# Turns of gathered rows bound behind a low part, a step sooner, and two more units by quarter rows: linear attention with a mixture of experts

## The chip, the cores and the metric

The kernel runs on one core of a Trainium2 chip. The metric is the device time of one execution in microseconds. Before the change it is 872.87 us, the median of three runs (872.1 to 873.55).

## The reference

```python
def phi(x):                                  # attention features, per head
    proj = x @ w_phi                         # 64 -> 128
    proj = proj - max(abs(proj), axis=-1)
    return concat([exp(proj), exp(-proj)])   # 256 features
q_p, k_p = phi(q), phi(k)                    # 8 x 8 heads, 576 tokens, head 64
x = (q_p @ (k_p.T @ v)) / (q_p @ sum(k_p) + 1e-6)      # -> [4608 tokens, 512]
logits = x @ w_gate                          # 8 experts
e = argmax(logits); gate = softmax(logits)[e]
out = gate * (relu(x @ w1[e]) @ w2[e])       # 512 -> 1024 -> 512, one expert per token
```

Everything is float32, with inputs and result of that type.

## The kernel before

The first part (up to about 400 us) computes the attention and writes its rows to `x_dram` in HBM, with the gate weights in `g_dram`. It also sorts the tokens by expert into blocks of 128, of which 41 are always computed. The second part runs the expert over these blocks. Blocks 0 to 37 go in pairs of one expert: pair unit `u` (0 to 18) holds blocks `2u` and `2u+1`. Blocks 38, 39 and 40 are the single units 19, 20 and 21.

Products keep float32 precision by splitting each operand into a high part (`wh`, `xh`, `hh`: a cast on ScalarE, ACT) and a low part (`wl`, `xl`, `hl`: a subtraction on VectorE, DVE), and by three matmuls on TensorE (PE): high by high, high by low, low by high. A pair unit has four steps `j` = 0 to 3. In each, `pair_first(u, j)` is 24 matmuls into the PSUM tile `pm` (two in flight), then `hh` on ScalarE and `hl` on VectorE; `pair_second` of the step before is 12 matmuls into `po`. A `po` matmul with `hl` (L1198) follows two that need `hh` alone. After the last step ScalarE scales both `po` by the gate into `ob`, and GpSimd (POOL) scatters them to `out`.

Rows of a block come to the tile `xg` (four of them) by indirect DMAs from POOL's queue. Early units take whole rows of 512 elements with one DMA per block (index `gidx`), later ones take a row in four quarters (index `qidx`), with four DMAs per block. `by_quarters(u)` says which. `x_parts(u, i)` then turns the block: without quarters by four PE transposes into the PSUM tile `px` (L1157), with quarters by one 32x32 block transpose on VectorE (L1152). From `px` come `xh` and `xl`.

In the loop over `u` the fetches for unit `u+2` are issued in unit `u`, divided over the steps by `cuts`; each waits for that step's `hh` (`paced`). `lined` keeps the order of row fetches and scatters in the pair loop as written. `behind(m, other)` only fixes that `m` stands after `other` on its engine. The rest of each engine's order is set by the scheduler that builds the program, by what is ready in its own model of time. So a turn of unit `u+2`, written in unit `u+1`, can stand one unit earlier than it is written, right behind its own fetches. Every engine runs its queue in order.

Of the kernel before, what the change touches and what calls it, by code (L numbers as in the profile page):

```python
# [14 lines left out]
ALU = mybir.AluOpType  # L15
# [30 lines left out]
KD = DM // P  # L46
# [10 lines left out]
def tile_linear_attention_moe(  # L57
# [12 lines left out]
    V, A, G, T = nc.vector, nc.scalar, nc.gpsimd, nc.tensor  # L70
# [189 lines left out]
    def behind(m, other):  # L260

        tc.add_manual_dep(
            m.ins,
            other.ins.name,
            mybir.DependencyInfo(mybir.DependencyClass.NoSync, mybir.DependencyReason.DATA),
            reason="order of the engine",
        )
# [796 lines left out]
    st = {}  # L1064
# [4 lines left out]
    def blocks(u):  # L1069
        return [2 * u, 2 * u + 1] if u < NPAIR else [u + NPAIR]  # L1070
# [13 lines left out]
    def weights(u, k):  # L1084

        if u >= lim[0] or ("w", u, k) in st:
            return
        if u > 0:
            load_weights(u, k)
        w = max(0, u - 1)  # L1090
        slot = f"{k}_{w % 2}" if k < KD else f"s{(w * (NPC - KD) + k - KD) % NSLOT}"
        pool = wp0 if slot == "s0" or (k < KD and w % 2 == 0) else wp1 if slot in ("s1", "s2", "s3") else wpr
        th = pool.tile([P, FF], F32R, name="wh", tag=f"wh{slot}")
        tl = pool.tile([P, FF], F32R, name="wl", tag=f"wl{slot}")
        A.copy(th, raw[k])  # L1095
        m = (G if k in (POOL_LO0 if u == 0 else POOL_LO if u >= NPAIR else ()) else V).tensor_tensor(tl, raw[k], th, op=ALU.subtract)  # L1096
        if (u, k) == (0, KD + 3):
            behind(m, st["places"])
        for j in range(2) if u == 0 else [u]:
            st["w", j, k] = (th, tl)  # L1100
        if u > 0:
            load_weights(u + 1, k)
        return m

    def by_quarters(u):
        return u >= 4

    def rows_of(b, u, step):
        st["xg", b] = gather_rows(gidx[:, b : b + 1], NT, st.get("experts"), step)
# [4 lines left out]
    def gather_steps(u):  # L1114
        if u >= lim[0]:
            return []
        steps = []
        for b in blocks(u):
            if ("xg", b) not in st:
                if b < NLEAD:  # L1120
                    st["xg", b] = early_rows[b]
                elif by_quarters(u):
                    steps += [lambda step, b=b, c=c: gather_quarter(b, c, step) for c in range(4)]
                else:
                    steps += [lambda step, b=b: rows_of(b, u, step)]
        return steps

    def gate_steps(u):
        if u >= lim[0]:
            return []  # L1130
        return [lambda step, b=b: gates_of(b, step) for b in blocks(u) if ("gate", b) not in st]
# [9 lines left out]
    def x_parts(u, i):  # L1141
        if u >= lim[0] or i >= len(blocks(u)) or ("x", u, i) in st:
            return
        if i == 0:
            st["x", u] = [mp.tile([P, KD, 2 * P], F32R, name=n) for n in ("xh", "xl")]
        st["x", u, i] = True
        xg = st["xg", blocks(u)[i]]
        px = ps_x.tile([P, KD, P], F32, name="px")
        xh, xl = (x[:, :, i * P : (i + 1) * P] for x in st["x", u])
        if by_quarters(u):  # L1150
            px = px.rearrange("p c (k t) -> p c k t", t=Q)
            V.transpose(px, xg.rearrange("p c (d k) -> p c k d", k=KD))  # L1152
            px = px.rearrange("p c k t -> p k c t")
            xh, xl = (x.rearrange("p k (c t) -> p k c t", t=Q) for x in (xh, xl))
        else:
            for k in range(KD):
                T.transpose(px[:, k, :], xg.rearrange("p c d -> p (c d)")[:, k : DM : KD], ident)  # L1157
        A.copy(xh, px)
        V.tensor_tensor(xl, px, xh, op=ALU.subtract)

    def first_weights(u, n, k):
        th, tl = st["w", u, 2 * n + k // 2]
        o = k % 2 * 512
        return th[:, o : o + 512], tl[:, o : o + 512]

    def pair_first(u, j, half=None):

        xh, xl = st["x", u]
        if half != 1:
            st["pm"] = ps_h.tile([P, 2, 2 * P], F32, name="pm")  # L1170
        pm = st["pm"]
        for i in range(2) if half is None else [half]:
            f = 2 * (j % 2) + i
            for k in range(KD):
                th, tl = (w[:, f * P : (f + 1) * P] for w in first_weights(u, j // 2, k))
                T.matmul(pm[:, i], th, xh[:, k, :], start=(k == 0), stop=False)  # L1176
                T.matmul(pm[:, i], th, xl[:, k, :], start=False, stop=False)  # L1177
                T.matmul(pm[:, i], tl, xh[:, k, :], start=False, stop=(k == KD - 1))  # L1178
        if half == 0:
            return  # L1180
        hh = mp.tile([P, 2, 2 * P], F32R, name="hh", bufs=4)
        hl = mp.tile([P, 2, 2 * P], F32R, name="hl", bufs=4)
        st["step"] = A.activation(hh, pm, AF.Relu)  # L1183
        V.scalar_tensor_tensor(hl, pm, 0.0, hh, op0=ALU.max, op1=ALU.subtract)  # L1184
        st["hp", u, j] = (hh, hl)

    def pair_second(u, j, half=None, between=()):
        if j == 0:
            pools = ((ps_o, "po") if u else (ps_t, "pht"), (ps_t, "pht"))
            st["po", u] = [p.tile([P, DM], F32, name="po", tag=t) for p, t in pools]  # L1190
        hh, hl = st["hp", u, j]
        th, tl = st["w", u, KD + j]
        for i in range(2) if half is None else [half]:
            for t, po in enumerate(st["po", u]):
                r, c = slice(t * P, (t + 1) * P), slice(i * DM, (i + 1) * DM)
                T.matmul(po, hh[:, i, r], th[:, c], start=(i == j == 0), stop=False)  # L1196
                T.matmul(po, hh[:, i, r], tl[:, c], start=False, stop=False)  # L1197
                T.matmul(po, hl[:, i, r], th[:, c], start=False, stop=(i == 1 and j == 3))  # L1198
        if j == 3 and half != 0:
            for i, (b, po) in enumerate(zip(blocks(u), st["po", u])):  # L1200
                write(b, po)
                for f in between if i == 0 else ():
                    f(None)
# [62 lines left out]
    for b in range(NLEAD):  # L1266
        st["xg", b] = early_rows[b]
    x_parts(0, 0)
    go(nums[:8])
    x_parts(0, 1)  # L1270
    go(nums[8:16])
    weights(0, 0)
# [5 lines left out]
    for b in range(NLEAD):  # L1278
        st["gate", b] = gather_gates(b, st["low"])
    run(r1[1:3])  # L1280
    pair_first(0, 0, 0)
    run(r2[:3])
    weights(0, 2)
# [5 lines left out]
    run(r2[3:4])  # L1289
    run(r1[4:])  # L1290
    pair_first(0, 0, 1)
    pair_first(0, 1, 0)
    pair_first(0, 1, 1)
    run(r2[4:])
# [15 lines left out]
    gather(2)  # L1310
    pair_second(0, 2)
    x_parts(1, 0)
    late.close()
    ps_o = ctx.enter_context(tc.tile_pool(name="ps_o", bufs=2, space=PSUM, side="left", reuse_waits="tile"))
# [10 lines left out]
    for u in range(1, NPAIR):  # L1325
        lining[0] = True
        fetches, extra = gather_steps(u + 2), gate_steps(u)
        n = len(fetches)
        cuts = (0, 1, 1, 2, 2) if n == 2 else (0, 2, 4, min(n, 6), n)
        parts = [fetches[a:b] for a, b in zip(cuts, cuts[1:])]  # L1330
        for j in range(4):
            pair_first(u, j)
            for f in (parts[0], parts[2], parts[3], ())[j]:
                f(st["step"])
            if j == 3:
                for f in extra:
                    f(st["step"])
            if j > 1:
                x_parts(u + 1, j - 2)
            if (u, j) != (1, 0):  # L1340
                pair_second(u - (j == 0), (j - 1) % 4, between=parts[1] if j == 0 else ())
            for du, k in AHEAD_W[j]:
                weights(u + du, k)
# [111 lines left out]
```

## Time and profile before

| what | value |
|---|---|
| median of three runs | 872.87 us (872.1 to 873.55) |
| the profiled execution, its own time | 873.48 us |
| span of its profile (first to last instruction) | 871.7 us |
| mean granted TensorE clock | 0.996 |
| PE busy | 859.9 us, 99% |
| VectorE, ScalarE, GpSimd busy | 71%, 66%, 63% |
| pair unit 1 | about 418 to 442 us |
| pair unit 18 | about 800 to 832 us |

In a row of the timeline the first number is the start in microseconds, the second the time taken; then engine, line, operation, output and inputs, sizes and count, and in brackets how long the engine had idled before and what ended that. A row of waits gives the total, the number of times and the longest. A row of groups or of a line's instructions gives the busy time and the mean, or the shortest, median and longest in nanoseconds. A busy matmul time overlaps that of its neighbours, so the distance between starts is what a matmul costs.

### The profile page before, as it was taken

What the parts mean: (1) busy time and instruction counts of PE and PEld (TensorE: products, weight loads), DVE (VectorE), ACT (ScalarE), POOL (GpSimd) and SP (SyncE); (2) the same over time, 40 slices, a digit from 0 to 9 for tenths busy, and PEclk for the clock granted to TensorE, in tenths of its full rate; (3) what the DMA queues carried; (4) which work ended last, traced back from release to release, by engine and by line L of the source; (5) the groups of instructions that cost most, each with busy time, mean ns of one, the idle gap of its engine ahead of it and who ended that gap; (6) DMA issues with size and microseconds to landing.
All of it is one profiled execution on the core that took longest, in us unless ns stands there. A gap on an engine that the chain in (4) does not pass through costs nothing. (4 is left out here: it accounts for less than half of the span.)

```text
span 871.7 us, 18059 instructions
## 1 busy us (share of the span) xinstructions
PE 859.9 (99%) x6605; PEld 807.1 (93%) x6605; DVE 623.0 (71%) x1044; ACT 571.3 (66%) x874; POOL 547.1 (63%) x407
## 2 busy tenths in 40 slices
PE   8999999999999999999999999999999999999897
PEld 6999999999999999999999999999999999999785
DVE  7688778887888788849857676766666666666451
ACT  5888888888788887753755555555555555555462
POOL 5677666876677767563456566566666566665762
PEclk9999999999999999999999999999999999999999
DMA  6233333523343334261352243432445644446550
GB/s 206 84 100 98 102 103 107 99 84 112 113 114 113 101 113 84 78 219 18 107 193 70 83 155 119 160 97 63 144 124 168 206 140 141 134 146 210 194 174 16
DMA packets 69692, 106.65 MB, mean 122 GB/s; under 512 B 13726, under 2 KB 31646, under 8 KB 69600
## 3 DMA queue, kind: packets, MB, share of 16 engines
q1 hardware_dynamic: 59312, 84.50, 32.3%
q0 software_dynamic: 9616, 20.81, 7.5%
q8 instruction: 53, 0.87, 0.4%
q14 instruction: 39, 0.32, 0.1%
q10 hardware_dynamic: 672, 0.15, 0.1%
HBM read 128.42 MB, written 20.26 MB: 171 GB/s over the span
## 5 line engine op out<-in xcount | busy, mean ns | idle before, releaser
L1095 ACT CAST wh<-raw 128x1024 fp32r<-128x1024 f32 x168 | 174.8, 1048 | 83.1 <-PE po L1198 34.9
L1096 DVE TENSOR_TENSOR wl<-raw,wh 128x1024 fp32r<-128x1024 f32 x160 | 196.1, 1238 | 42.5 <-ACT wh L1095 33.1
L889 POOL DMA_INDIRECT xg<-x_dram,qidx x132 | 152.1, 1152 | 83.6 <-ACT hh L1183 49.0
L476 PE MATMUL pn<-kf,qp 128*128 128x73 f32 (+1 forms) x1152 | 185.1, 255 | 0.0
L476 PEld LDWEIGHTS pn<-kf,qp 128*128 128x128 f32 x1152 | 172.0, 190 | 0.5
L1178 PE MATMUL pm<-xh,wl 128*128 128x256 f32 x608 | 172.3, 283 | 0.0
L1177 PE MATMUL pm<-xl,wh 128*128 128x256 f32 x608 | 172.1, 283 | 0.0
L1176 PE MATMUL pm<-xh,wh 128*128 128x256 f32 x608 | 171.6, 282 | 0.0
L341 POOL TENSOR_TENSOR kl<-e,kh 128x1024 fp32r<-128x1024 f32 x45 | 107.4, 2387 | 98.8 <-ACT kh L339 98.8
L313 DVE TENSOR_REDUCE mx<-ps_proj 128x4 f32<-128x512 f32 (+1 forms) x160 | 100.8, 632 | 50.8 <-PE ps_proj L309 48.8
L1198 PE MATMUL po<-wh,hl 128*128 128x512 f32 x304 | 119.2, 393 | 2.6 <-DVE hl L1184 2.6
L1196 PE MATMUL po<-wh,hh 128*128 128x512 f32 x304 | 120.2, 396 | 0.0
L1197 PE MATMUL po<-wl,hh 128*128 128x512 f32 x304 | 119.8, 394 | 0.0
L1176 PEld LDWEIGHTS pm<-xh,wh 128*128 128x128 f32 x608 | 116.4, 191 | 2.9
L1177 PEld LDWEIGHTS pm<-xl,wh 128*128 128x128 f32 x608 | 116.4, 191 | 2.8
L1178 PEld LDWEIGHTS pm<-xh,wl 128*128 128x128 f32 x608 | 116.4, 191 | 0.1
L314 DVE TENSOR_TENSOR t<-ps_proj,mx 128x512 f32<-128x512 f32 (+1 forms) x160 | 101.0, 634 | 4.5
L1152 DVE STREAM_TRANSPOSE px<-xg 128x512 f32<-128x512 f32 x33 | 37.0, 1124 | 93.6 <-DMA xg<-x_dram,qidx 91.3
L255 POOL TENSOR_TENSOR xl<-xr,xh 128x640 fp32r<-128x640 f32 (+1 forms) x60 | 96.8, 1630 | 9.4 <-ACT xh L254 8.8
L406 PE MATMUL pk<-kh,vl 128*64 128x256 f32 x300 | 101.4, 338 | 0.0
L406 PE MATMUL pk<-kl,vh 128*65 128x256 f32 x300 | 99.8, 333 | 0.0
L406 PE MATMUL pk<-kh,vh 128*65 128x256 f32 x300 | 99.3, 331 | 0.0
(217 smaller groups left out, 1910.7 us busy)
## 6 DMA issues: line engine op xcount, KB each, us to landing
raw<-w SPq DMA_DIRECT2D x168, 512.0 KB
vt<-vv SPq DMA_DIRECT2D x15, 640.0 KB
x_dram<-xrow SPq DMA_DIRECT2D x30, 256.0 KB
xr<-kT SPq DMA_DIRECT2D x15, 320.0 KB
xr<-qT SPq DMA_DIRECT2D x15, 320.0 KB
xr<-kT SPq DMA_DIRECT2D x17, 256.0 KB
xr<-qT SPq DMA_DIRECT2D x17, 256.0 KB
xg<-x_dram,qidx POOLq DMA_INDIRECT x132
```

The costliest lines, as they stand in the source:

```text
L341: eng.tensor_tensor(kl, e[:, 0:m], kh, op=ALU.subtract)
L406: return T.matmul(st["pk", bb][0:n, hh, :], (vl if j == 1 else vh)[:, 2 * (c + (bb if c == 8 else 0)) + hh, 0:n], (kl if j == 2 else kh)[: ...
L476: m = T.matmul(pn[:, i - a, :] if c < 8 else pn[:, 2 + hh : 6 : 2, :], qp[:, s, s0 + hh, :], st["kf"][:, hh, s, c // 4, :] if c < 8 else s ...
L889: m = G.indirect_dma_start(out=out, out_offset=None, in_=source[0:rows], in_offset=bass.IndirectOffsetOnAxis(ap=index, axis=0), bounds_che ...
L1095: A.copy(th, raw[k])
L1096: m = (G if k in (POOL_LO0 if u == 0 else POOL_LO if u >= NPAIR else ()) else V).tensor_tensor(tl, raw[k], th, op=ALU.subtract)
L1176: T.matmul(pm[:, i], th, xh[:, k, :], start=(k == 0), stop=False)
L1177: T.matmul(pm[:, i], th, xl[:, k, :], start=False, stop=False)
L1178: T.matmul(pm[:, i], tl, xh[:, k, :], start=False, stop=(k == KD - 1))
L1196: T.matmul(po, hh[:, i, r], th[:, c], start=(i == j == 0), stop=False)
L1197: T.matmul(po, hh[:, i, r], tl[:, c], start=False, stop=False)
L1198: T.matmul(po, hl[:, i, r], th[:, c], start=False, stop=(i == 1 and j == 3))
```

## The change

The change has four parts. A turn on VectorE is bound to stand behind the latest `hl` (`st["low part"]`). The parts of unit `u+1` are written in steps 1 and 2 of unit `u` and no longer in steps 2 and 3. Units 2 and 3 (blocks 4 to 7) are fetched by quarters and turned on VectorE too. The fetches of unit 3, now eight, are divided over the steps of unit 1 by `cuts` of their own.

```diff
     def by_quarters(u):
-        return u >= 4
+        return u >= 2
...
         if by_quarters(u):
             px = px.rearrange("p c (k t) -> p c k t", t=Q)
-            V.transpose(px, xg.rearrange("p c (d k) -> p c k d", k=KD))
+            m = V.transpose(px, xg.rearrange("p c (d k) -> p c k d", k=KD))
+            if st["low part"] is not None:
+                behind(m, st["low part"])
...
-        V.scalar_tensor_tensor(hl, pm, 0.0, hh, op0=ALU.max, op1=ALU.subtract)
+        st["low part"] = V.scalar_tensor_tensor(hl, pm, 0.0, hh, op0=ALU.max, op1=ALU.subtract)
...
-        cuts = (0, 1, 1, 2, 2) if n == 2 else (0, 2, 4, min(n, 6), n)
+        cuts = (0, 3, 3, 6, n) if u == 1 else (0, 2, 4, min(n, 6), n)
...
-            if j > 1:
-                x_parts(u + 1, j - 2)
+            if j in (1, 2):
+                x_parts(u + 1, j - 1)
```

All lines behind the second hunk move down by two. What follows is the order in which instructions stand in an engine's queue.

VectorE in unit 18, before, from its `hl` of step 1 on. `px_11283` and `px_11380` are the turns of blocks 39 and 40; their `xg` tiles are filled in unit 18 itself.

```order
L1184 SCALAR_TENSOR_TENSOR hl_11062<-pm_11036,hh_11061 128x512
L1096 TENSOR_TENSOR wl_11205<-raw1_5818,wh_11204 128x1024
L1152 STREAM_TRANSPOSE px_11283<-xg_10991 128x512
L1152 STREAM_TRANSPOSE px_11380<-xg_11303 128x512
L1184 SCALAR_TENSOR_TENSOR hl_11115<-pm_11089,hh_11114 128x512
L1096 TENSOR_TENSOR wl_11345<-raw4_5824,wh_11344 128x1024
L1096 TENSOR_TENSOR wl_11252<-raw2_5820,wh_11251 128x1024
```

The same place with the change: `px_11091` is the turn of block 38 (its `xg` is filled in unit 17), `px_11307` and `px_11404` are those of blocks 39 and 40.

```order
L1186 SCALAR_TENSOR_TENSOR hl_11086<-pm_11060,hh_11085 128x512
L1152 STREAM_TRANSPOSE px_11091<-xg_10759 128x512
L1096 TENSOR_TENSOR wl_11229<-raw1_5818,wh_11228 128x1024
L1161 TENSOR_TENSOR xl_11090<-px_11091,xh_11089 128x4x128
L1186 SCALAR_TENSOR_TENSOR hl_11145<-pm_11119,hh_11144 128x512
L1096 TENSOR_TENSOR wl_11369<-raw4_5824,wh_11368 128x1024
L1096 TENSOR_TENSOR wl_11276<-raw2_5820,wh_11275 128x1024
L1186 SCALAR_TENSOR_TENSOR hl_11205<-pm_11179,hh_11204 128x512
L1152 STREAM_TRANSPOSE px_11307<-xg_11015 128x512
L1152 STREAM_TRANSPOSE px_11404<-xg_11327 128x512
```

The turns of blocks 39 and 40 moved from ahead of the `hl` of step 2 to behind that of step 3. In units 4 to 17 each turn moved in the same way, by nearly a unit.

GpSimd's queue in unit 1, before. Behind the computing of `eg` (the experts of the blocks) come the whole rows of blocks 4 and 5, the scatters of unit 0, the rows of blocks 6 and 7 and the gate row of block 3.

```order
L1059 TENSOR_TENSOR eg<-eg,iota_p 1x352
L889 DMA xg<-x_dram,gidx 128x512 x2
L1248 DMA out<-ob,sidx_74 4608x512 x2
L889 DMA xg<-x_dram,gidx 128x512 x2
L889 DMA gate<-g_dram,gidx 128x4
```

The same place with the change:

```order
L1059 TENSOR_TENSOR eg<-eg,iota_p 1x352
L889 DMA xg<-x_dram,qidx 128x128 x8
L1250 DMA out<-ob,sidx_74 4608x512
L889 DMA xg<-x_dram,qidx 128x128 x2
L1250 DMA out<-ob,sidx_74 4608x512
L889 DMA xg<-x_dram,qidx 128x128 x6
L889 DMA gate<-g_dram,gidx 128x4
```

The gate row of block 3 stands behind 18 DMAs and no longer behind 6. VectorE in unit 1 gets the two turns of blocks 4 and 5, behind the `hl` of steps 1 and 2; on PE 16 transposes are gone, four each at steps 2 and 3 of units 1 and 2.

## The prediction

> **What bounds the kernel now.** I read the page's busy times first, then the waits of PE, then those of VectorE (DVE), then the order of time around the one long wait of PE.
>
> ```profile
> PE 859.9 (99%) x6605; PEld 807.1 (93%) x6605; DVE 623.0 (71%) x1044; ACT 571.3 (66%) x874; POOL 547.1 (63%) x407
> PE po L1198 <- DVE hl L1184: 2.6, 1, 2.6
> DVE px L1152 <- DMA xg<-x_dram,qidx: 91.3, 29, 8.3
> ```
>
> PE is the bound: it has work in 859.9 of 871.7 us, and after the start it waits for something only once, 2.6 us for a low part `hl`. VectorE waits far longer, 91.3 us in 29 waits, always in front of a turn (`px`) whose gathered rows have not landed. Nearly all of that is VectorE's own slack. So a saving must come from work that leaves PE, or from that one wait. The wait lies in the last pair unit (18):
>
> ```profile
> 820.22 2.12 DVE L1152 STREAM_TRANSPOSE px<-xg 128x512 f32<-128x512 f32 x2 [8.32 <-DMA xg<-x_dram,qidx]
> 822.23 0.69 DVE L1184 SCALAR_TENSOR_TENSOR hl<-pm,hh 128x512 fp32r<-128x512 f32 x1
> 815.26 0.60 ACT L1183 ACTIVATE hh<-pm 128x512 fp32r<-128x512 f32 x1 [2.77 <-PE pm L1178]
> ...
> 815.73 0.39 PE L1197 MATMUL po<-wl,hh 128*128 128x512 f32 x1
> 816.64 0.39 PE L1198 MATMUL po<-wh,hl 128*128 128x512 f32 x1
> 819.97 0.40 PE L1197 MATMUL po<-wl,hh 128*128 128x512 f32 x1
> 822.97 0.67 PE L1198 MATMUL po<-wh,hl 128*128 128x512 f32 x1 [2.60 <-DVE hl L1184]
> 826.72 0.40 PE L1198 MATMUL po<-wh,hl 128*128 128x512 f32 x1
> 800.00:819.00 19.00, 19.00 (x127) 17.52 (x126) 8.48 (x7) 9.14 (x11) 13.70 (x11) 1.00 0.75 254
> 822.80:826.60 3.80, 3.63 (x9) 2.86 (x10) 3.80 (x5) 0.00 (x0) 3.31 (x4) 0.55 0.06 12
> ```
>
> The high part `hh` that this `hl` needs was done at 815.26 + 0.60 = 815.86. VectorE could have made `hl` by 816.5. It stood in its queue behind two turns, of blocks 39 and 40, and the first of them waited 8.32 us for rows. PE wanted `hl` at about 820.2 and got it at 822.9. Behind the wait the matmuls start 0.43 us apart and not 0.23, and the last two rows (stretches of time; busy time of PE, PEld, DVE, ACT, POOL, then the granted clock) give a clock of 1.00 up to 819 and of 0.55 behind the wait.
>
> **The change, part by part.**
>
> *The bond and the earlier step.* Every turn now stands behind the `hl` of its step, for rows that were asked for one unit earlier. In unit 18 the turns of blocks 39 and 40 come after the unit's last `hl` (first piece of the order). Between `hl` of step 1 and of step 2 stands now only the turn of block 38, whose rows are asked for in unit 17, some 20 us before. So `hl` is ready near 816.5 against a need at 820.2, and the wait has nothing left to stand on. Its price, from starts: ten matmuls from 819.97 to 826.72 took 6.75 us. At the usual distance, (816.64 - 815.73) / 4 = 0.2275 us, they take 2.28. The difference is **4.47 us**: 2.77 for the wait (822.97 - 819.97 - 0.23) and 1.70 for the half clock behind it.
>
> The Trainium skill (TensorE: Matmul & The Clock Gate, "What's actually happening") has the array go back to half rate after at least one idle window of about 3.4 us, and says that this window runs freely. The trace shows half rate behind an idle time of 2.60 us, shorter than that. If one held to the page, this stretch would not hang on this wait, 1.70 us would stay, and the saving on the wait would be 2.77; I keep the rows' reading, because the slow starts begin with the first matmul behind the wait.
>
> Is the tail able to follow? What comes after is PE's own:
>
> ```profile
> 830.00:866.00 36.00, 35.41 (x168) 28.91 (x166) 13.91 (x15) 18.99 (x27) 14.78 (x10) 1.00 0.32 97
> 815.74 0.99 POOL L889 DMA_INDIRECT xg<-x_dram,qidx  x1 [0.30 <-issue]
> 820.05 0.59 ACT L1183 ACTIVATE hh<-pm 128x512 fp32r<-128x512 f32 x1
> 835.15 0.39 PE L1212 MATMUL pm<-wh,xh 128*128 128x512 f32 x1
> ```
>
> PE is busy 35.41 of the last 36 us, so an earlier start moves the end. The late turns find their rows: the last quarter is issued at 815.74 and the first turn began at 820.22, so they had landed by then, while the last `hl` before them ends near 820.05 + 0.59 + 0.69 = 821.3. Two turns (2.12 us) and `xl` of block 39 are done by about 825. PE needs that `xl` at the third matmul of its product, 835.15 + 0.45 - 4.5 = 831.1. What is late next is thus 6 us early, and I take zero loss.
>
> *Units 2 and 3 by quarters.* Four blocks (4 to 7) are no longer turned on PE. Each of the four looks like this one:
>
> ```profile
> 429.53 0.28 PE L1177 MATMUL pm<-xl,wh 128*128 128x256 f32 x1
> 429.65 0.28 PE L1178 MATMUL pm<-xh,wl 128*128 128x256 f32 x1
> 429.77 0.65 PE L1157 MATMUL px<-ident,xg 128*128 128x128 f32 x4
> 430.50 0.39 PE L1197 MATMUL po<-wl,hh 128*128 128x512 f32 x1
> L1157 PE MATMUL px<-ident,xg 128*128 128x128 f32 x16 | 2.6, 286 | 0.0
> ```
>
> From the last `pm` to the second `po` it is 430.50 - 429.65 = 0.85 us. Without the turn it would be one `pm` distance (429.65 - 429.53 = 0.12) and one `po` distance (0.23), 0.35. So 0.50 us per block, **2.0 us** for four, where PE waits for nothing (the 16 matmuls of the last row have no idle time before them).
>
> What it adds: four turns on VectorE, 4 x 1.12 us, and 16 quarter fetches on GpSimd's queue (POOL) where 4 whole ones stood. These fall into unit 1, past other work on both queues. VectorE first:
>
> ```profile
> L1152 DVE STREAM_TRANSPOSE px<-xg x33: 1095/1122/1170, 458.9 to 821.2; 128x512 f32<-128x512 f32 x33
> 424.98 0.69 DVE L1184 SCALAR_TENSOR_TENSOR hl<-pm,hh 128x512 fp32r<-128x512 f32 x1 [0.53 <-ACT hh L1183]
> 425.59 5.75 DVE L1096 TENSOR_TENSOR wl<-raw,wh 128x1024 fp32r<-128x1024 f32 x5
> 431.26 0.68 DVE L1184 SCALAR_TENSOR_TENSOR hl<-pm,hh 128x512 fp32r<-128x512 f32 x1
> 431.86 0.68 DVE L1159 TENSOR_TENSOR xl<-px,xh 128x512 fp32r<-128x512 f32 x1
> 436.85 0.40 PE L1198 MATMUL po<-wh,hl 128*128 128x512 f32 x1
> 439.25 0.28 PE L1177 MATMUL pm<-xl,wh 128*128 128x256 f32 x1
> ...
> 417.48 1.04 POOL L889 DMA_INDIRECT xg<-x_dram,gidx  x1 [0.16 <-issue]
> L889 POOL DMA_INDIRECT xg<-x_dram,qidx x132: 991/1035/1963, 443.1 to 815.7; - x132
> L889 POOL DMA_INDIRECT xg<-x_dram,qidx x132 | 152.1, 1152 | 83.6 <-ACT hh L1183 49.0
> 772.59 1.00 POOL L889 DMA_INDIRECT xg<-x_dram,qidx  x1 [0.30 <-issue]
> 775.37 1.13 DVE L1152 STREAM_TRANSPOSE px<-xg 128x512 f32<-128x512 f32 x1 [3.36 <-DMA xg<-x_dram,qidx]
> ```
>
> The first new fetch starts at 417.48. One every 1.152 + 0.30 = 1.45 us (mean and usual gap), and landing 1.8 us after the issue ends (775.37 against 772.59 + 1.00), puts block 4's fourth quarter at 417.48 + 3 x 1.45 + 1.15 + 1.8 = 424.8 and block 5's at 430.6. The turns stand behind `hl` of steps 1 and 2, which end at 425.7 and about 432, so neither waits. Between these two `hl` there were five `wl` (5.75 us); now a turn, an `xl` and four `wl`, 1.12 + 0.68 + 4.6 = 6.4, so the second `hl` ends near 432.6. PE needs it at 436.85 - 1.0 = 435.85 (two turns gone ahead of it). `xl` of block 5 ends near 435.7; PE needs it at 439.25 - 1.0 = 438.25. Margins of 2.5 us and more: cost zero. At the slowest pace of any quarter (1.96 + 0.30 each) block 5 lands at 436.3 and `xl` is ready at 436.3 + 1.12 + 1.15 + 0.68 = 439.3 (a `wl`, 5.75 / 5, stands between), a loss of 1.0 us. Bounds 0 and 1.0; I take 0, since mean and median lie at the fast end.
>
> POOL second. The gate row fetch of block 3 stood behind 6 DMAs counted from 417.48 and started at 437.06; it now stands behind 18 (second piece of the order). ScalarE's second `ob` of unit 1 needs it, and what is queued there behind `ob` is `hh` of unit 2:
>
> ```profile
> 437.06 1.36 POOL L889 DMA_INDIRECT gate<-g_dram,gidx  x1 [7.11 <-ACT hh L1183]
> 444.28 1.37 ACT L1246 ACTIVATE ob<-po,gate 128x512 f32<-128x512 f32 x2 [1.47 <-issue]
> 446.99 1.05 ACT L1095 CAST wh<-raw 128x1024 fp32r<-128x1024 f32 x1 [0.41 <-issue]
> 454.21 0.40 PE L1198 MATMUL po<-wh,hl 128*128 128x512 f32 x1
> ```
>
> At 1.45 us each the gate starts at 417.48 + 18 x 1.45 = 443.6 and lands at 446.6, about 2.6 us later than `ob` would run (444.96 less 1.0). From there: `ob` 0.69, two casts 2.1, `hh` 0.60, `hl` 0.68, ready at 450.7. PE needs it at 454.21 - 1.5 = 452.7. So the gate may land as late as 448.6 for nothing; I take zero, and this is the tightest place. At 1.29 us each (the fastest quarter and the gap) it lands at 443.7; at 2.26 each at 461.1, 12.5 us too late. The mean is nearer to the fast end.
>
> *Everywhere else* (units 4 to 17) the turns move behind `hl` and find rows of the unit before. This takes VectorE's 91.3 us of waiting away, which PE did not feel. A bound upward: the only trace of those waits on PE outside unit 18 would be a stall, and its list of waits has none. The counts of `xh` and `xl` stay; ScalarE's `xh` stands right behind its turn's step, and VectorE's `xl` one or two rows behind the turn, so it costs VectorE at most one `xh` (0.59) of idle time per block.
>
> **The sum.** 4.47 + 2.0 = 6.5 us. The profiled execution took 873.48 us (span 871.7), 0.6 over the median 872.87 of the runs. 873.48 - 6.5 = 867.0; against the median **866.4 us**. No more can be hoped for than about a microsecond beyond: PE has no other wait. The three runs lie 0.7 to either side of their median, so about 0.2% (1.7 us) can be told from no change.
>
> **The rivals.**
>
> *The gate row comes late (slower).* Place: ScalarE's second `ob` at the start of unit 2. Price: one us of PE for each us past 448.6, and 1.7 more if the clock halves. It decides when the loss reaches 6.5, a landing at 448.6 + 4.8 = 453.4, a mean pace of (453.4 - 2.95 - 417.48) / 18 = 1.83 us per DMA. For it: 18 DMAs in one row, each of 512-byte rows. Against: mean 1.45, median 1.34. With a pace of 2.0, the gate lands at 456.4 and the time is 866.4 + 7.8 + 1.7 = 875.9. At 1.65 it lands at 450.1, costs 1.5, and the time is 868.
>
> *The half clock stays.* By that the clock drops for another reason near 820 and only 2.77 + 2.0 goes: 868.1. Against: the granted clock is 1.00 right up to the wait. This is what the Trainium skill's clock gate rule, held to the letter, would give.
>
> *The bond does not free `hl`.* Some other work holds it there until the same time, and only the 2.0 of the turns comes: 870.9. For it: the rows of blocks 39 and 40 still come through the same POOL queue. Against: in the new order no turn that waits for them stands ahead of an `hl` of unit 18.
>
> **How the numbers follow.** Forecast 0.80 (866.4, own range 865.4 to 867.6). Half clock stays 0.04. `hl` not freed 0.05. Gate late 0.11: 0.06 with a loss under 4.7, 0.02 about even, 0.03 slower. The range from 865.0 (0.7 of spread and the small gaps below) to 869.5 (half clock, the 1.0 of block 5, a gate up to 3 late) leaves some 0.1 to 0.15 out. Faster by over 0.2%: 0.80 + 0.04 + 0.06 + half of the 0.05, about 0.92. Within: 0.05. Slower: 0.03.
>
> **What would show it.** Right: no wait of PE for `hl` near 818, granted clock 1.00 there; `po` steps of 0.23 us right through unit 18; 16 matmuls of L1159 on PE and not 32; 37 turns on VectorE with almost no wait for `xg`. Wrong: a wait of PE in 430 to 460 for `hl` or `xl`, an `ob` of unit 1 waiting for its gate past 448, or a new wait between 815 and 860.

## The result, and the profile after

The changed kernel is slower. In the runs beside the kernel before it takes 878.1 us (median of 6, 876.8 to 879.8) against 872.6 (median of 6), a ratio of 1.0059 with a 95% interval from 1.0043 to 1.0075. The forecast was 866.4, with 865.0 to 869.5 as its range. The profiled execution took 879.75 us, with a span of 877.7 at a clock of 0.994.

First the rows of the profile after that answer to those of before: busy times, the turns on PE and on VectorE, PE's waits behind 400 us and the head of VectorE's waits.

```profile
PE 861.9 (98%) x6589; PEld 807.5 (92%) x6589; DVE 630.4 (72%) x1048; ACT 570.3 (65%) x874; POOL 562.0 (64%) x419
L1159 PE MATMUL px<-ident,xg x16: 270/285/387, 382.6 to 417.4; 128*128 128x128 f32 x16
L1152 DVE STREAM_TRANSPOSE px<-xg x37: 1081/1094/1147, 437.7 to 832.2; 128x512 f32<-128x512 f32 x37
...
PE pm L1179 <- issue: 3.3, 5, 0.9
PE pm L1180 <- issue: 1.2, 2, 0.8
PE po L1198 <- issue: 0.7, 1, 0.7
...
DVE wl L1096 <- ACT wh L1095: 58.2, 58, 3.4
DVE hl L1186 <- ACT hh L1185: 51.6, 30, 9.3
```

What was to come came: 16 transposes on PE, 37 turns on VectorE, no wait of VectorE for `xg` (91.3 us before), no wait of PE for `hl`. New is that PE waits for "issue", that is for nothing that the profile shows, and that VectorE once waits 9.3 us for an `hh`. The place is unit 1. Two blocks of four stretches each (busy time and count of PE, PEld, VectorE, ScalarE, POOL, then granted clock): first the kernel before, then the changed one.

```profile
418.00:424.00 6.00, 6.00 (x50) 5.92 (x49) 4.21 (x5) 5.52 (x7) 2.54 (x3) 1.00 0.45 134
424.00:430.00 6.00, 6.00 (x41) 5.51 (x40) 5.47 (x6) 5.79 (x8) 4.20 (x3) 1.00 0.27 90
430.00:436.00 6.00, 6.00 (x41) 5.50 (x40) 5.94 (x7) 3.40 (x5) 0.00 (x0) 1.00 0.37 130
436.00:442.00 6.00, 6.00 (x41) 5.50 (x40) 4.78 (x5) 3.27 (x5) 1.36 (x1) 1.00 0.28 92
```

```profile
418.00:424.00 6.00, 6.00 (x47) 5.80 (x46) 3.38 (x4) 3.60 (x5) 4.78 (x5) 1.00 0.17 46
424.00:430.00 6.00, 4.92 (x24) 3.44 (x23) 1.91 (x2) 2.48 (x3) 4.73 (x5) 1.00 0.16 45
430.00:436.00 6.00, 2.54 (x10) 1.92 (x10) 0.00 (x0) 0.00 (x0) 4.08 (x4) 0.78 0.32 113
436.00:442.00 6.00, 5.66 (x23) 5.01 (x23) 4.93 (x6) 5.56 (x7) 3.00 (x3) 0.65 0.15 42
```

From 430 to 436 PE has 10 matmuls where 41 stood, and VectorE and ScalarE have nothing. POOL alone goes on. The timeline of PE, ScalarE and POOL in the changed kernel:

```profile
429.47 0.28 PE L1178 MATMUL pm<-xh,wh 128*128 128x256 f32 x1
430.65 0.28 PE L1179 MATMUL pm<-xl,wh 128*128 128x256 f32 x1 [0.89 <-issue]
430.76 0.29 PE L1180 MATMUL pm<-xh,wl 128*128 128x256 f32 x1
430.89 0.28 PE L1178 MATMUL pm<-xh,wh 128*128 128x256 f32 x1
432.08 0.28 PE L1179 MATMUL pm<-xl,wh 128*128 128x256 f32 x1 [0.91 <-issue]
...
424.96 0.60 ACT L1185 ACTIVATE hh<-pm 128x512 fp32r<-128x512 f32 x1 [3.24 <-PE pm L1180]
436.44 0.60 ACT L1185 ACTIVATE hh<-pm 128x512 fp32r<-128x512 f32 x1 [9.00 <-remote]
...
417.94 1.03 POOL L889 DMA_INDIRECT xg<-x_dram,qidx  x1 [0.16 <-issue]
434.22 1.02 POOL L889 DMA_INDIRECT xg<-x_dram,qidx  x1 [0.31 <-issue]
437.31 1.00 POOL L889 DMA_INDIRECT xg<-x_dram,qidx  x1 [2.06 <-ACT hh L1185]
```

From the first to the second of the three POOL rows, both counted, POOL issues 13 indirect DMAs with 0.30 us from one to the next and no other pause. From 429 to 433 PE begins three matmuls, then none for about 1.2 us, then three again, and the profile shows no data that they wait for. The first gap is of another kind: PE's `po` at 425.61 follows the end of an `hh` (424.96 + 0.60 = 425.56). That `hh` came 2.7 us late: it started at 421.66 in the kernel before, and unit 1 begins only 0.6 us later here. VectorE's long idle time is a wait for ScalarE too, so what stands still of itself here is PE and ScalarE. About 1 us after the run's last DMA ends at 435.24 everything moves again. From 433.3 on the clock is at half for 6.8 us.

Where the time went can be read from starts: where the last `po` matmul of a unit stands, against the kernel before (us; minus is earlier; worked out from the profiles' matmul starts).

| kernel | unit 0 | unit 1 | unit 2 | first `po` of unit 18 | unit 18 | span |
|---|---|---|---|---|---|---|
| changed | +0.6 | +8.6 | +7.6 | +7.4 | +4.7 | +6.0 |
| bond and step alone (e1) | +0.4 | +0.4 | +0.4 | +0.2 | -4.3 | -4.1 |
| bond, step, unit 3 by quarters (j2) | -0.2 | -0.3 | -1.3 | -1.0 | -5.5 | -4.8 |

In the changed kernel unit 1 adds 8.0 although two blocks' transposes (1.0 us) are gone there, so the loss is 9.0; unit 2 gives back 1.0 for its two blocks; unit 18 gives back 2.7, since a second, smaller stutter of 1.8 us (also "issue") lies at 824 to 826, at the end of another run of 9 DMAs (its size differs between profiles: 3.0 in i1, 0.6 in j1 of the experiments); and behind the last matmul the program ends 1.3 us later than before.

That last part goes with the number of indirect DMAs in the program, whatever the chip. From the last matmul's start to the end it is 6.7 us in the three profiles with 222 of them (before, e1, g2 of the experiments), 7.4 in the seven with 228 (one unit more by quarters), 8.0 to 8.1 in the nine with 234 (both units, and h2) and 10.4 in the one with 252 (e4). That is 0.11 to 0.13 us for each. Most of it is one step of GpSimd's queue at the end of the program, the longest `DRAIN` (rows: the kernel before, the changed one):

```profile
L1451 POOLq DRAIN  x3: 40/107/1467, 869.4 to 871.4; - x3
L1453 POOLq DRAIN  x3: 40/107/2447, 874.4 to 877.4; - x3
```

### The profile page after: what moved, and what is told of

It is laid out like the page before. It is cut to its first block, busy times and chain, and to the rows that moved or that the text cites. A ratio compares the mean times of both kernels' runs of the same rounds, so it can differ in the third digit from the quotient of the medians.

```text
span 877.7 us, 18076 instructions
## 1 busy us (share of the span) xinstructions
PE 861.9 (98%) x6589; PEld 807.5 (92%) x6589; DVE 630.4 (72%) x1048; ACT 570.3 (65%) x874; POOL 562.0 (64%) x419
## 5 line engine op out<-in xcount | busy, mean ns | idle before, releaser
L889 POOL DMA_INDIRECT xg<-x_dram,qidx x148 | 171.0, 1155 | 85.4 <-ACT hh L1185 47.3
L1185 ACT ACTIVATE hh<-pm 128x512 fp32r<-128x512 f32 x76 | 45.4, 598 | 80.1 <-PE pm L1180 66.1
```

The costliest lines, as they stand in the source:

```text
L889: m = G.indirect_dma_start(out=out, out_offset=None, in_=source[0:rows], in_offset=bass.IndirectOffsetOnAxis(ap=index, axis=0), bounds_che ...
```

## The experiments

Short names: *bond* is `behind(m, st["low part"])`, *step* is the parts written in steps 1 and 2. "Excess" is what the distances between PE's matmul starts add up to beyond the median distance of their kind, over the stretch named, worked out from the profile.

### First runs: which part costs the time

Edits, each against the changed kernel or the one before:

```diff
e1_bond_step (changed kernel):        return u >= 4; cuts of before
e2_unit3_quarters (changed kernel):   return u >= 3
e3_quarters_only (kernel before):     return u >= 2; cuts of the change
e4_runs (e1), behind the gate rows of units 5, 8, 11, 14:
+    for i in range({5: 3, 8: 6, 11: 9, 14: 12}.get(u, 0)):
+        extra_rows = wpr.tile([P, P], F32, name="spare_rows", bufs=3)
+        m = fetch_rows(extra_rows, <quarters of x_dram>, qidx[:, i % 4, 6:7], 4 * NT)
+        paced(m, st["step"])
```

e1: 

> The bond and the earlier step alone; units 2 and 3 are gathered by whole rows again, as before. Theory A (the loss of the changed kernel comes from the unbroken run of 13 indirect DMAs on POOL between 417.9 and 435.3 us, while which PE and ACT get their instructions too slowly): no loss in unit 1, the 4.5 us of unit 18 are kept, about 868.4 us. Theory B (the loss comes from the turn being one step earlier and tied behind the low part, so that VectorE and with it PE wait in unit 1): the loss stays, 876 us or more.

e2: 

> As the changed kernel, but only unit 3 (blocks 6 and 7) goes over to quarter rows; unit 2 (blocks 4 and 5), whose eight quarters were issued without a pace at the head of the run, keeps its two whole-row gathers. Theory A: the run on POOL in unit 1 is broken up (6 indirect DMAs fewer in it), no loss there, and half of the 2.0 us of the transposes is added to the 4.5: about 867.4 us. Theory B: 876 us or more, as with the changed kernel. If a run of 6 is enough to starve PE, between the two: 870 to 874.

e3: 

> The kernel before with quarter rows for units 2 and 3 and the new cuts, without the bond and without the earlier step. Theory A: the loss in unit 1 is there (about 10 us), the 2.0 us of the transposes are saved, and the wait of unit 18 stays: about 880 us. Theory B: no loss in unit 1, about 870.9 us.

e4: 

> The kernel of the first experiment with additional quarter-row gathers into spare rows that nothing reads, issued back to back behind the gate rows of four pair units: 3 in unit 5, 6 in unit 8, 9 in unit 11 and 12 in unit 14. Theory A: PE shows gaps put down to issue once POOL has run for some 7 to 11 us without a break, so none in unit 5, some at 6 and more, growing with the number: 5 to 20 us in all over the first experiment. Theory B (turns on VectorE): the time of the first experiment within 1 us, since these gathers delay no turn.

Measured: e1 869.0 us (ratio 0.9949, 0.993 to 0.9968). e2 868.6 (0.9945, 0.9924 to 0.9967). e3 879.3 (1.0061, 1.0038 to 1.0083). e4 891.9 (1.0212, 1.0174 to 1.025).

Theory B falls: bond and step without the new quarter rows gain their 4.3 us. e2 gains only 0.4 over e1, although two blocks' turns (1.0 us) are gone from PE; its program ends 0.8 us later behind the last matmul, with six more indirect DMAs. e3 met the number of theory A, and e4 lost 22.9 us against e1, near the 5 to 20 that theory A gave. But both did so by other causes, as their profiles show. In e3 the bond is missing, and a turn stands ahead of a low part again, now in unit 1 (VectorE's row, then the wait of PE):

```profile
424.85 1.11 DVE L1152 STREAM_TRANSPOSE px<-xg 128x512 f32<-128x512 f32 x1 [5.67 <-DMA xg<-x_dram,qidx]
PE po L1198 <- DVE hl L1184: 3.4, 1, 3.4
```

In e4 the additional gathers made gate rows late: ScalarE waits for them, with `hh` queued behind (waits from 690 to 800). Where no gate was late, from 596 to 642, 30 indirect DMAs stood in one unbroken run, and the third row has PE busy all through it:

```profile
ACT ob L1248 <- DMA gate<-g_dram,gidx: 24.7, 3, 12.9
...
596.00:642.00 46.00, 46.00 (x295) 41.87 (x294) 30.21 (x32) 24.62 (x33) 35.96 (x30) 1.00 0.41 131
```

So an unbroken run alone does not empty PE, and theory A as I had written it falls too. What told the profiles apart was SP. It waits for nothing while it works out the addresses of the weights and issues their loads (L1081), and its steps are short. Rows: shortest, median and longest step in ns, from 418 to 437; first the changed kernel, then e3, which has the same eight gathers at the same place:

```profile
L1081 SPq ALU_OP  x14: 3/39/698, 418.9 to 436.5; - x14
L1081 SPq MOVE raw<-w x11: 2/16/692, 419.3 to 436.8; - x11
```

```profile
L1081 SPq ALU_OP  x19: 34/38/55, 419.0 to 435.8; - x19
L1081 SPq MOVE raw<-w x14: 29/29/37, 419.3 to 436.0; - x14
```

In the changed kernel a register step takes up to 0.7 us, of whatever kind, again and again. I call this the standstill. e1 to e4 ran on one chip (13); which chip the changed kernel's first profile comes from is not on record.

### Second and third group: the program or the chip

f1, g1 are the changed kernel unedited, g2 is e1, g3 is e3. f3 is the changed kernel with

```diff
-        return u >= 2
+        return u == 2 or u >= 4
```

and the cuts of before. f1: 

> The changed kernel itself, unedited, profiled a second time. In its first profile SP, PE, ACT and VectorE all stand still for some 0.5 to 0.7 us at a time between 419.8 and 435.7 us, while in the kernel with quarter rows alone (e3_quarters_only) SP runs freely beside the same run of gathers. Theory C (the standstill belongs to this program): about 878 us again, with SP's steps of 0.5 to 0.7 us in the same place. Theory D (it belongs to the first profile and its chip): SP runs freely and unit 1 has no gap of PE put down to issue; about 866.5 us, the forecast, or, if a real wait is behind it, a time that a wait of PE for hh, hl or xl in unit 1 explains.

f3: 

> As the changed kernel, but only unit 2 (blocks 4 and 5) goes over to quarter rows; unit 3 keeps two whole-row gathers and the cuts of before. Theory A (the eight quarters of unit 2, issued without a pace at the head of unit 1, cost the time, whatever follows them): loss of some 10 us in unit 1, about 877 us. Theory A2 (the eight of unit 2 and those of unit 3 are needed together, in one run of 13): no loss, and 1.0 us under the kernel with bond and step alone (e1_bond_step, 869.0), so about 868.

g1: 

> The changed kernel, the bond and step alone, and the quarter rows alone, once more on one chip, with a profile of each: the two kernels whose profile shows SP standing still (the changed one and f3_unit2_quarters) and the three whose profile does not were run on different chips. This one is the changed kernel. Theory C (the standstill belongs to the program): 878 to 879 us, with SP's steps of 0.5 to 0.7 us from 419 to 436. Theory E (it belongs to the chip): either all three profiles of this call show such steps beside their gathers, or none does; if none does, unit 1 of the changed kernel has no gap put down to issue and it takes 866 to 868 us.

g2: 

> The bond and the earlier step alone, as in e1_bond_step. Theory C: 869 us, no step of SP over 0.45 us beside the gathers. Theory E, on a chip with the standstill: steps of 0.5 to 0.7 us beside the runs of gathers in the middle units, and a time of 869 to 872; on a chip without: as e1_bond_step, 869.

g3: 

> Quarter rows and cuts alone, as in e3_quarters_only: there a turn stood ahead of a low part on VectorE and PE waited 3.5 us in unit 1 for it. Theory C: 879 us for that wait and that of unit 18, SP free. Theory E, on a chip with the standstill: the standstill in unit 1 on top of it, up to 885 us; on a chip without: 879 again.

Measured on chip 10: f1 879.3 (1.0068, 1.0054 to 1.0082), f3 877.1 (1.005, 1.0037 to 1.0064). On chip 0: g1 879.8 (1.007, 1.0046 to 1.0095), g2 870.4 (0.9966, 0.9945 to 0.9986), g3 883.0 (1.0098, 1.0064 to 1.0132).

f1 shows the gaps again, at the same times within half a microsecond, so the loss is no accident of one profile. f3 shows that the eight gathers of unit 2 are enough for most of it. And the pairs e1/g2 and e3/g3, one program each on two chips, tell that the standstill goes with the chip (or with something else that the runs of one group share): steps of SP over 0.45 us between 405 and 860, register loads left out, are 0 in e1 and 24 in g2, 1 in e3 and 26 in g3. The row of g2 against that of e1, 418 to 437:

```profile
L1081 SPq FUSED_REGOPS  x26: 2/50/551, 418.7 to 437.0; - x26
```

```profile
L1081 SPq FUSED_REGOPS  x27: 37/50/56, 418.9 to 435.8; - x27
```

Theory E holds in this form. Over all runs chips 13 and 3 give 0 or 1 such steps in eight kernels, chips 10, 0, 5 and 4 give 20 to 31 in ten; the profile of the kernel before has 9, that of the changed one 30. The same program costs 1.4 us more on chip 0 than on 13 (g2, a stutter of 1.0 at 818 in its profile), and 3.8 more (g3).

### Fourth group: breaking the run

h1 is f3 with block 5's four gathers held back, h4 the same with all quarter rows and unit 3's cuts at (0, 0, 0, 3, n); h2 is e4 with {5: 2, 8: 4, 11: 6}; h3 is e2.

```diff
-    gather(2)
+    later = gather_steps(2)
+    for f in later[:4]:
+        f(None)
...
             pair_first(u, j)
+            if (u, j) == (1, 0):
+                for f in later[4:]:
+                    f(st["step"])
```

h1: 

> As f3_unit2_quarters (only unit 2 by quarter rows, 877.1 us there), but block 5's four quarters are held back until hh of the first step of unit 1, so that the run of eight is cut into four and four with a pause between. Theory F (PE lives for some 10 us on instructions it already has while POOL issues gathers back to back; only a longer run empties it): no gap put down to issue in unit 1, about 868.5 us. Theory G (the quarter rows of unit 2 cost the time in any order): 875 to 878.

h2: 

> The bond and step alone, with 2, 4 and 6 additional quarter gathers into spare rows behind the gate rows of units 5, 8 and 11 (in e4_runs 3 and 6 did nothing to PE, 9 and 12 made the gate rows late). Theory F on a chip with the standstill: no gap at 2, 0.5 to 1.5 us of gaps at 4, more at 6, all beginning 9 us or more behind the head of a run: 871 to 876 us in all. On a chip without it, and by theory G: within 1 us of the bond and step alone.

h3: 

> The kernel of e2_unit3_quarters (bond, step, unit 3 alone by quarter rows) beside the others on this chip: 868.6 us on chip 13. Theory F: on a chip with the standstill its run in unit 1 begins with whole rows of 2 us each, so no gap put down to issue, 868.5 to 870. Theory G: the same.

h4: 

> All quarter rows, bond and step of the changed kernel; block 5's four quarters wait for hh of the first step of unit 1, unit 3's for hh of the second (3) and third (5). A first run of four or five, a pause, then one of some 14 gathers from about 425 to 443. Theory F on a chip with the standstill: gaps only from about 435 on, 3 to 6 us instead of 9: 871 to 875. On a chip without it 866 to 868. Theory G: 878 to 880.

Measured, all on chip 3: h1 869.8 (0.997, 0.996 to 0.9979), h2 871.8 (0.9992, 0.9982 to 1.0002), h3 868.8 (0.9959, 0.9945 to 0.9973), h4 871.4 (0.9992, 0.9982 to 1.0001).

Chip 3 has no standstill, so these runs could not decide between F and G. They show what the delay itself costs. h1 is 1.3 us above the 868.5 that was expected, h2 2.8 us above e1 (expected within 1), h4 3.4 us above the upper end of its 866 to 868. In h2 and h4 ScalarE waits for gate rows (the two rows: h2 from 690 to 710, h4 from 435 to 456), and in h1 the turn of block 5 waits 3.8 us for its rows, with 0.7 us of it on PE:

```profile
ACT ob L1248 <- DMA gate<-g_dram,gidx: 7.0, 2, 6.2
ACT ob L1248 <- DMA gate<-g_dram,gidx: 5.9, 1, 5.9
```

So with 18 DMAs ahead of it in unit 1 the gate row can come late after all, once the gathers of block 5 and of unit 3 wait for a later `hh`. In h3's expectation I was wrong on what its run consists of: it is unit 3's eight quarters, not whole rows (the expectation of j2 below has the same mistake).

### Fifth group: one long run and a divided one on one chip

i1 is the changed kernel, i2 is f3, i3 is h1. i1: 

> The changed kernel once more, beside f3_unit2_quarters and h1_split on one chip. On a chip with the standstill (SP's steps of 0.5 to 0.7 us beside gathers): 878 to 880. On a chip without: theory E says no gap in unit 1 put down to issue and 866 to 868 us; theory C (it belongs to the program) 878 and the gaps as before.

i2: 

> The kernel of f3_unit2_quarters (bond, step, unit 2 alone by quarter rows, its eight gathers without a pace). On a chip with the standstill 876 to 878, with PE's gaps from 424 on; on one without, by theory E, 868.

i3: 

> The kernel of h1_split (the same gathers, cut into four and four by a pace): 869.8 on a chip without the standstill. Theory F on a chip with it: 869 to 871, that is 6 us or more under the kernel with the eight in one run on this chip. Theory G: the same time as that kernel, 876 to 878.

Chip 5 has the standstill. Measured: i1 879.4 (1.0063, 1.0039 to 1.0086), i2 876.0 (1.0028, 1.0014 to 1.0042), i3 871.2 (0.9975, 0.9959 to 0.9992). Two stretches of each, in that order:

```profile
424.00:430.00 6.00, 4.83 (x23) 3.31 (x21) 1.92 (x2) 2.48 (x3) 4.61 (x4) 1.00 0.17 45
430.00:436.00 6.00, 3.00 (x9) 2.00 (x10) 0.00 (x0) 0.00 (x0) 4.08 (x4) 0.75 0.35 118
```

```profile
424.00:430.00 6.00, 4.27 (x19) 3.19 (x20) 1.92 (x2) 2.48 (x3) 4.78 (x5) 1.00 0.20 66
430.00:436.00 6.00, 4.82 (x24) 4.49 (x24) 2.47 (x3) 3.10 (x5) 2.46 (x3) 0.72 0.42 119
```

```profile
424.00:430.00 6.00, 5.11 (x30) 4.07 (x29) 4.38 (x5) 5.47 (x8) 3.12 (x3) 1.00 0.24 89
430.00:436.00 6.00, 6.00 (x42) 5.51 (x41) 4.99 (x6) 4.33 (x6) 5.09 (x4) 1.00 0.12 33
```

i2 and i3 have the same gathers, turns and matmuls, and differ in one pace. i3's first run ends after five DMAs:

```profile
417.44 1.03 POOL L889 DMA_INDIRECT xg<-x_dram,qidx  x1 [0.16 <-issue]
422.69 1.02 POOL L1250 DMA_INDIRECT out<-ob,sidx  x1 [0.30 <-issue]
426.27 1.93 POOL L1250 DMA_INDIRECT out<-ob,sidx  x1 [2.56 <-ACT wh L1095]
```

PE's excess in and behind the first run is 1.4 us for this run of 5 (6.3 us), 5.6 for i2's of 10 (13.4 us), 8.8 for i1's of 13 (17.4 us). The time of the whole falls by 4.9 us from i2 to i3. Theory G falls: the same quarter rows cost far less when one pace divides them. Theory F has the direction right, though it gave 6 us or more, and its figure of 10 us is wrong for unit 1, where a high part `hh` is late after 6.6 us; at 9 DMAs near 820 the first gap stands 10.3 us behind the run's head (i1).

But the length of the run isn't the whole condition. The middle units of the same profiles have runs as long that cost nothing. In i2 the first row is unit 1's run of ten, the others a later run of ten and two of its DMAs:

```profile
417.00:430.40 13.40, 11.57 (x73) 9.87 (x71) 5.38 (x6) 6.09 (x8) 10.66 (x10) 1.00 0.20 61
673.50:687.70 14.20, 14.20 (x92) 12.90 (x92) 8.94 (x10) 7.22 (x10) 11.43 (x10) 1.00 0.70 221
678.78 2.04 POOL L889 DMA_INDIRECT xg<-x_dram,qidx  x1 [0.30 <-issue]
685.09 1.35 POOL L889 DMA_INDIRECT xg<-x_dram,qidx  x1 [0.30 <-issue]
```

The eleven profiles that show the standstill (the changed kernel's first, f, g, i and j) have 42 runs of ten behind 405 us, worked out from POOL's rows. The two in unit 1 (f3, i2) begin with seven DMAs of at most 1.2 us each, and PE's excess up to 1.5 us behind their end is 4.4 us. In the other 40 no more than four such quick DMAs stand in a row, and the excess is 0.2 us at most. Of 109 runs of eight, six are quick throughout; they cost 0.4 to 1.3 us each, the others 0.1 at most. So what goes with the loss is a run of quick DMAs. i3's pace also puts its later gathers beside work of VectorE, where they are slower, so length and quickness are not told apart by an edit.

### Sixth group: the best version on such a chip

j1 is the changed kernel, j2 is e2. j1: 

> The changed kernel. On a chip with the standstill 878 to 880 us with PE's gaps from 424 to 436. On a chip without it: 866 to 868 if the unbroken run costs nothing there (theory E); 878 if the run costs the same everywhere and the two free chips were free only because no such run was tried on them.

j2: 

> Bond, step, and unit 3 alone by quarter rows (e2_unit3_quarters; 868.6 and 868.8 us on the two chips without the standstill). On a chip with it: no gap in unit 1, since its run there begins with whole rows; up to 1.5 us at the tail, as the bond and step alone had there, so 868.6 to 870.5. On a chip without it 868.7.

Measured on chip 4, which has the standstill: j1 879.7 (1.0067, 1.0048 to 1.0086), j2 868.6 (0.9948, 0.9934 to 0.9961). j2 beats both kernels, and with e2 and h3 it has the same time on three chips of both kinds. Its unit 1, and two DMAs of its run of ten:

```profile
424.00:430.00 6.00, 6.00 (x41) 5.50 (x40) 5.42 (x7) 5.91 (x8) 4.52 (x4) 1.00 0.19 63
430.00:436.00 6.00, 6.00 (x41) 5.50 (x40) 6.00 (x7) 3.39 (x5) 5.09 (x4) 1.00 0.18 54
...
425.87 1.04 POOL L889 DMA_INDIRECT xg<-x_dram,qidx  x1 [0.30 <-issue]
427.21 1.95 POOL L889 DMA_INDIRECT xg<-x_dram,qidx  x1 [0.30 <-issue]
```

PE begins 41 matmuls in each stretch. That its run of ten did no harm goes, I think, with its pace: it takes 16.5 us, since some gathers take up to 1.97 us while VectorE works; in i2 VectorE stands still and ten take 13.4. The runs in the middle units agree with that reading; no edit has tested it.

What stays open: what holds the engines on those chips, and what the changed kernel takes on a chip without the standstill. It was profiled five times and always met the kind that has it.

## Why the prediction was wrong

*The bond and the earlier step, 4.47 us: right.* In e1 unit 18 goes from +0.2 to -4.3, in j2 from -1.0 to -5.5: 4.5 us. The clock is 1.00 there in both, so the half clock went with the wait, against the rival that it stays. In the changed kernel 1.8 of it are lost again to the stutter.

*The turns, 0.50 us per block: right on PE, but a cost beside it was left out.* Unit 2 gives 1.0 for two blocks in the changed kernel and in j2. The sum has no term for the end of the program, where the 12 additional indirect DMAs take 1.3 of the 2.0 us back, on any chip. Even without the loss in unit 1 the forecast would thus have been about 1.3 us too low.

*VectorE in unit 1, zero: right in itself.* The turns stood where the order put them and waited for no row.

*POOL in unit 1, zero: this is the step that failed.* I priced the 18 DMAs by when their rows and the gate row land: the gate row was to start at 443.6. It started at 447.9, behind three waits for an `hh` that the sum had left out, and the second `ob` of unit 1 still found it. But the loss had come before, by 437, beside the run of 13 DMAs (that such a run causes it is shown on the shorter one of i2, which one pace mends in i3). I had counted what stands behind those DMAs on POOL's own queue and in the rows they bring, and nothing that they could do to engines that wait for neither. The term was 9.0 us (and 1.8 in unit 18), where I wrote zero. What holds the engines is open.

*The rivals.* None of the three was this one. A late gate row, the slower one, is real (e4, h2, h4), but not in the changed kernel. *What would show it wrong* named a wait for `hl` or `xl` between 430 and 460; the wait came there, but for issue.

Could it have been seen? In the profile of before SP's steps have the sign of it, within a run of three gathers and a scatter, at a cost of nothing:

```profile
L1081 SPq FUSED_REGOPS  x27: 3/50/563, 418.6 to 436.0; - x27
```

One step of 563 ns stands there against a median of 50. I had read SP's issues and not the lengths of its steps. Its longest runs of gathers, 10 in 14.3 to 15.7 us, cost PE nothing, which would have spoken against.

## What to carry to other kernels

An indirect DMA on GpSimd's queue has a price beside its own time. Here each one added 0.11 to 0.13 us at the end of the program. And on some chips other engines stand still for half a microsecond and more at a time beside a run of gathers; PE bore five quick ones with 1.4 us of loss, thirteen DMAs with 8.8. So don't issue many small gathers in one quick row without a pace; where they must be early, take whole rows, as the version with unit 2 by whole rows and unit 3 by quarters does (868.6 us, of which all but 0.4 comes from bond and step). And when an experiment reaches the number that a theory gave, read its profile before taking the theory: e3 met it for another reason.

## What was not expected of the hardware

- On chips 10, 0, 5 and 4 (and in the changed kernel's first profile) SP, PE and ScalarE get on only in pieces while POOL issues quick indirect DMAs in unit 1: register steps of SP with a median of 13 to 56 ns take up to 0.70 to 0.72 us there (1.28 in f3), and PE begins three matmuls per DMA. On chips 13 and 3 nothing of it is seen, not even beside 30 DMAs in a row. The Trainium skill (Runtime: NRT & Kernel Launch, "Instruction fetch mechanics") says that each engine's sequencer fetches its instructions ahead by a DMA queue of its own and that this is mostly hidden. In the changed kernel's unit 1 the trace has packets of the instruction queues at 421.9, 427.4 and 438.4 and none from 428 to 438, so no such transfer is under way while PE stands. What holds the engines no run shows.
- The profile gives ScalarE's second `hh` of unit 1 at 436.44 "remote", although the matmuls of its `pm` are recorded up to 424.9. Either the signal or the record is late; the same is seen in f1 and i1.
- A gather of quarter rows takes 1.00 us while VectorE is idle and up to 1.97 (j2), 2.54 (i3) in unit 1 while it makes a `wl`. In five profiles (the changed kernel's first, i2, i3, j1, j2) all 364 indirect DMAs of over 1.2 us overlap a `wl`, and none of the 431 that overlap none takes as long. The Trainium skill (SBUF — State Buffer, "SBUF: two separate sides") has a port pair that VectorE and GpSimd share, held by one instruction at a time; a VectorE operation with two SBUF inputs holds it only against a GpSimd operation that reads SBUF. `wl` has two such inputs, and the rows agree in direction. Here it may have helped, since it stretches the run.
- The half clock of PE comes in pieces: 3.4 us in the kernel before, 6.8 in the changed one (433.3 to 440.2).
